# A causal attention kernel's opening, written out slot by slot with fewer weight blocks, and one product for a pair's diagonals

## The chip, the cores and the metric

The kernel runs on one core of a Trainium2 chip. The metric is the device time of one execution in microseconds (us). TensorE is called PE below, VectorE DVE, ScalarE ACT, GpSimd POOL, and SyncE (which issues the DMAs) SP.

## What is computed

Attention with a decaying causal bias on q, k, v of 4 batches, 8 heads, 576 tokens and 64 columns, then two MLPs on the 2304 tokens of 512 columns, with 2048 hidden columns each:

```python
scores = scale * np.matmul(q, k.transpose(0, 1, 3, 2))
cum = np.cumsum(np.log(np.clip(f, 0.0001, 1.0)), axis=-1)
decay = cum[:, :, :, None] - cum[:, :, None, :]
scores = np.where(causal, -1000000000.0, scores + decay)
scores = scores - np.max(scores, axis=-1, keepdims=True)
attn = np.exp(scores)
attn = attn / (np.sum(attn, axis=-1, keepdims=True) + 1e-09)
x = np.matmul(attn, v)                      # then to (tokens, 512)
h = np.maximum(x @ w_in, 0.0)
x = (s * (h * h) + b) @ w_out               # first MLP
h = x @ w_in2
return np.maximum(0.01 * h, h) @ w_out2     # second MLP
```

All inputs are fp32.

## The kernel before

**Units.** The attention is cut into eight units: the first 256 rows of each of the four batches (units 0 to 3), then the other 320 rows of each. A unit has four pairs of heads. For a pair of one of the first units the steps are: S, the scores on PE (q times k, L663 in unit 0 and L300 in units 1 to 3; in unit 0 the decays too, L672; and the mask, L678 or L311); M, the row maxima on DVE (reductions, L684, in unit 0, where the decays are already in the scores; a custom instruction that adds the decays and takes the maximum, L334, in the others); E, the exponentials on ACT with their row sums (L690, L356); D, on DVE, a small addition and a reciprocal (L701 and L702, or L381 and L382) and the diagonal matrices with the reciprocals in them (L715, a product of 128 by 128 for each head and row tile, four for a pair); T, the turn, in which PE multiplies the exponentials by the diagonals and so transposes and scales them at once (L725, twelve products of 128 by 128 for a pair) and ACT copies the result (L710, L387); A, the product with v (L734, eight products); X, the split of the result into a high part (ACT, L748) and a low part (DVE, L749), which is written to `x_all`.

**Weights.** A block of weights (512 KB) is loaded by SP and converted in four instructions or groups: a scaling on ACT (`scale`, L109), a join of three instructions on DVE (`join`, L113, L114, L116), a rounding to the high part on ACT (`high`, L122) and the subtraction of it on DVE (`low`, L126). Each MLP has 32 blocks.

**Stages.** The opening does units 0 and 1, from the start to the first Relu of the first MLP (L952), and converts the first weight blocks on the way. Then come 16 joint steps, which do the first MLP for units 0 and 1 together (L937, L987, 512 columns wide) with unit 2's attention and the rest of the weights' conversion in between. The next units go one by one: in each step one sixteenth of the first MLP of a unit and a piece of a later unit's attention (`attend`, `attend_mid`, `first_mlp`). The second MLP (L1071, L1087) is last.

**What sets the order.** In the opening Tile's scheduler orders each engine by priorities (`ahead`, `run_on`): `first_a`, `first_b`, `first_c` issue S with M and E, D with T, and A with X of unit 0, `first_slots` those of unit 1, so that the two units are interleaved, and `split_to` issues conversions at the lowest priority. From the joint steps on, `in_order` fixes the order on each engine as it is written. There the diagonals of a pair (`diags`, four small instructions and four products) stand at the start of the step after the one that took its exponentials:

```python
        dg.update({k: diags(k) for k in e["turn"]})
```

and the pair's turn stands in that step behind the first product of the MLP (behind the second one in a unit's first step). `W_FIRST` 4, `W_LOAD` 3 and `W_MOST` 18 say how many weight blocks are loaded in the opening; `c_of` says which blocks a joint step converts, from block 8 on, two in a step and one in each third.

Of the kernel before, what the change touches and what calls it, by code (L numbers as in the profile page):

```python
# [8 lines left out]
F32 = mybir.dt.float32  # L9
# [30 lines left out]
def attention_moe_moe_kernel(  # L40
# [51 lines left out]
    class Weights:  # L92
# [35 lines left out]

        def split_to(self, n):
            for k in range(self.done, min(n, len(self.blocks))):  # L130
                self.scale(k)
                self.join(k)
                self.high(k)
                self.low(k)
# [135 lines left out]
    def run_on(first):  # L270
        return nullcontext() if first else tc.high_priority(offset=P_RUN)

    def mm_score(i):

        jb, n, ts, last = tiles[i]
        u, h, j, half = jobs[jb]
        if not half and h % 2:
            return
        b, u0, un, _ = units[u]
        qk = qk_p[j // 2]  # L280
        qn = q_cols(u)
        ps = s_t[i] = ps_a.tile([P, 2, 512], F32, tag="ps_s", name="ps_s", bufs=1)
        if half:
            w = (u0 + un) // 2
            for c in range(2):
                with run_on(c == 0):
                    nc.tensor.matmul(
                        ps[:, c, :w], qk[:, UN:qn], qk[:, qn + c * w : qn + (c + 1) * w], start=True, stop=c == 0
                    )
            with run_on(False):  # L290
                nc.tensor.matmul(ps[:, 1, w - NL : w], ident_h, mask_l, start=False, stop=True)
            return
        s_t[i + 1] = ps
# [26 lines left out]
    def score_max(i):  # L320
# [4 lines left out]
        sm = sm_t[i] = ap.tile([P, 10], F32, tag="sm", name="sm", bufs=4)  # L325
# [39 lines left out]
    def st_split(i):  # L365
        jb, n, ts, last = tiles[i]
        dg = diags(i)
        ps = ps_o.tile([P, 512], F32, tag=f"o{2 + i % 2}", name="ps_t1")
        turn(ps, t_t.pop(i), dg)
        p_t[i] = turned(i, ps)  # L370

# [7 lines left out]
    def diags(i):  # L379
        sm = sm_t.pop(i)  # L380
        nc.vector.tensor_scalar(sm[:, 4:6], sm[:, 2:4], 1.0e-9, None, ALU.add)  # L381
        nc.vector.reciprocal(sm[:, 6:8], sm[:, 4:6])  # L382
        return row_parts(i), diag(i, {t: sm[:, 6 + r : 7 + r] for r, t in enumerate(tiles[i][2])})
# [50 lines left out]
    kept = {}  # L434
# [4 lines left out]

    def st_av(i):  # L440
        jb, n, ts, last = tiles[i]
        u, h, j, half = jobs[jb]
        b, u0, un, _ = units[u]
        if h % 2:
            first_x(u, h // 2, pair_av(u, i))
# [5 lines left out]
    def av_mm(i):  # L451
# [7 lines left out]
        for t in ts:  # L459
# [3 lines left out]
            for e in range(P // m):  # L463
                for k in range(nk):
                    for l in range(2):
                        with run_on(t == ts[0] and e == k == l == 0):
                            nc.tensor.matmul(  # L467
                                av[:, at + e * m : at + (e + 1) * m],
                                v_st[j + e][:, k].rearrange("p l d -> p (l d)"),
                                pt[:, to + l * nk + k, e * m : (e + 1) * m],  # L470
                                start=(k == 0 and l == 0),
                                stop=(k == nk - 1 and l == 1),
                            )
# [25 lines left out]
    def av_end(i):  # L499
# [16 lines left out]
    def split_later():  # L516
        while later and later[0][0] <= read[0] + 2:
            u, pr, raw, inv = later.pop(0)
            with ahead(P_X):
                split_x1(xs[u], pr, raw, inv)  # L520
# [25 lines left out]
    P_ATT, P_AV, P_G, P_W, P_F, P_X = 150, 90, 0, -300, 0, 100  # L546
    P_RUN = 4000

    def ahead(n):
        return tc.high_priority(offset=n)  # L550

    LAG = 2
    NCUM = 3
    U1 = 2
    W_FIRST = 4
    W_LOAD = 3
    W_MOST = 18
    XL = 10

    def slot_c(i):  # L560
        if 0 <= i - 1 < NTL:
            st_split(i - 1)

    def slot_d(i):
        if 0 <= i - LAG < NTL:
            st_av(i - LAG)

    def slot_b(i):
        if i < NTL:
            jb, n, ts, last = tiles[i]  # L570
            st_score(i)
# [9 lines left out]
    qk_0 = []  # L581
    f_sb = ap.tile([P, S], F32, tag="tt", name="f_sb", bufs=4)[:BH]
    cum = ap.tile([P, S], F32, tag="tt", name="cum", bufs=4)[:BH]
    nc.sync.dma_start(out=f_sb, in_=f)
    nc.scalar.preload_act_table_set("natural_log_exp_and_others")
    for r in range(ND // 2):
        qk_0.append(wp.tile([P, 2, 2 * un0], F32, tag="w", name="qk_0"))
        for e in range(2):
            nc.sync.dma_start(out=qk_0[r][:, e], in_=qk0[2 * r + e])
        if r == 0:  # L590
            for _ in range(W_FIRST):
                w1.load(nc.sync)
# [15 lines left out]
    cl = wp.tile([P, 2 * DM], F32R, tag="w", name="cum_hl")  # L608
    for a in range(P // BH):
        nc.gpsimd.tensor_scalar(  # L610
            cl[a * BH : (a + 1) * BH, S : S + H],
            ident[a * BH : (a + 1) * BH, a * BH : a * BH + H],
            -INV,
            0.0,
            ALU.mult,
            ALU.add,
        )
    nc.gpsimd.tensor_copy(ident_h, ident)
    nc.gpsimd.memset(mask_h, 0.0)
    nc.gpsimd.affine_select(  # L620
        out=mask_h,
        in_=mask_h,
        pattern=[[-1, P]],
        compare_op=ALU.is_ge,
        fill=MASK,
        base=0,
        channel_multiplier=1,
    )
    nc.gpsimd.memset(mask_l, 0.0)
    for e in range(2):  # L630
        nc.gpsimd.affine_select(
            out=mask_l[e * D : (e + 1) * D],
            in_=mask_l[e * D : (e + 1) * D],
            pattern=[[-1, NL]],
# [5 lines left out]
    nc.vector.tensor_scalar(f_sb, f_sb, 1.0e-4, 1.0, ALU.max, ALU.min)  # L640
    nc.scalar.activation(f_sb, f_sb, AF.Ln)
    nc.vector.tensor_tensor_scan(cum, f_sb, f_sb, 0.0, ALU.add, ALU.bypass)
    nc.scalar.copy(cl[:BH, :S], cum)
    nc.vector.tensor_tensor(
        out=cl[BH : 2 * BH, :S], in0=cum, in1=cl[:BH, :S].bitcast(F32), op=ALU.subtract
    )
    nc.gpsimd.tensor_scalar(f_sb, cum, -INV, 0.0, ALU.mult, ALU.add)
    nc.sync.dma_start(out=cumd, in_=f_sb)
    nc.gpsimd.tensor_scalar(cl[D:, :un0], cl[:D, :un0].bitcast(F32), 1.0, 0.0, ALU.mult, ALU.add)

    e_0, sm_0, pt_0 = {}, {}, {}
    xs.update({u: x_all[:, u % 2] for u in range(NU)})

    def first_a(p):
        qk = qk_0[p // 2][:, p % 2]
        ps = [ps_o.tile([P, 512], F32, tag=f"o{e}", name="ps_s0") for e in range(2)]
        ex = e_0[p] = wp.tile([P, 2 * DM], F32, tag="w", name="e_0")
        sm = sm_0[p] = ap.tile([P, 5, 2 * NT0], F32, tag="sm_0", name="sm_0", bufs=3)
        parts = [(t, P * t * (t + 1) // 2, (t + 1) * P, e) for t in range(NT0) for e in range(2)]
# [664 lines left out]
```

## Time and profile before

| what | value |
| --- | --- |
| median of 3 runs | 1014.13 us (1011.58 to 1014.45) |
| the profiled execution | 1013.08 us |
| its span in the profile | 1011.2 us |
| PE busy | 982.7 us (97%) |
| DVE busy | 528.4 us (52%) |
| ACT busy | 507.0 us (50%) |
| POOL busy | 27.7 us (3%) |
| PE's mean granted clock | 0.998 of full |

Busy time is the time in which an engine executes an instruction; a share is of the whole span, over stages that differ. Where PE is busy all the time, only its own work counts; in a stage where it isn't, the wait that ends last before each of its instructions does. In a timeline's row the bracket behind an instruction gives the idle time of its engine before it and what ended it. The granted clock is a share of PE's full speed: 1.00 is 2.4 GHz, 0.50 is 1.2 GHz.

### The profile page before, as it was taken

Reading aid. Unit: us, or ns where it says so; the run is one execution under the profiler, and the core shown is the slowest. Engines: PE = TensorE matmul, PEld = TensorE weight load, DVE = VectorE, ACT = ScalarE, POOL = GpSimd, SP = SyncE. Lnnn points to the kernel's source line nnn. Section 1 sums busy time; section 2 is a strip of 40 time slices with the busy share of each in tenths; the row PEclk is TensorE's granted clock in tenths of the full one; section 3 lists DMA queues with packets and bytes.
Section 4 is the critical chain, followed back from the end, with each engine's and each line's share of the span. In section 5 each row is a group of like instructions: output and inputs, shape, how many; then the busy total and the mean of one; then the engine's idle time right before and its main releaser. Section 6 shows DMA issues by size and latency. Waiting matters only on the chain.

```text
span 1011.2 us, 17155 instructions
## 1 busy us (share of the span) xinstructions
PE 982.7 (97%) x6464; PEld 836.5 (83%) x6464; DVE 528.4 (52%) x1383; ACT 507.0 (50%) x1196; POOL 27.7 (3%) x100
## 2 busy tenths in 40 slices
PE   5899999999999999999999999999999999999998
PEld 4667777888888888888999998888888888888887
DVE  6888774367777777777512479785112111211121
ACT  4777665567667677676643556552121222212132
POOL 1000000000000000000000000000000000000000
PEclk9999999999999999999999999999999999999999
DMA  9834022379999899898400695003000100100010
GB/s 298 301 124 174 22 84 84 90 130 199 173 188 201 178 177 202 171 182 186 87 22 1 214 376 202 0 1 123 3 1 1 63 0 1 42 1 1 1 42 21
DMA packets 157075, 110.32 MB, mean 109 GB/s; under 512 B 110593, under 2 KB 135169, under 8 KB 156993
## 3 DMA queue, kind: packets, MB, share of 16 engines
q1 hardware_dynamic: 156992, 109.23, 42.9%
q8 instruction: 51, 0.84, 0.3%
q14 instruction: 32, 0.25, 0.1%
HBM read 74.00 MB, written 10.04 MB: 83 GB/s over the span
## 4 chain that ended last, share of the span: by engine, by line
PE 51%; ACT 0%; DVE 0%; issue 0%
PE ps_o L1087 20%; PE ps_h L1071 20%; PE ps_o L987 6%; PE ps_h L937 6%; PE ps_v L467 0%; DVE o L1099 0%; ACT tt L356 0%; ACT p_hl L410 0%; DVE g L970 0%; ACT g L968 0%; ACT ps_h L967 0%; ACT ps_h L966 0%
## 5 line engine op out<-in xcount | busy, mean ns | idle before, releaser
L937 PE MATMUL ps_h<-x_all,w 128*128 128x256 f32 (+1 forms) x1536 | 231.7, 299 | 2.3 <-ACT r_all L952 0.7
L987 PE MATMUL ps_o<-g,w 128*128 128x256 f32 (+2 forms) x1536 | 231.3, 300 | 0.0
L1087 PE MATMUL ps_o<-w,g 128*128 128x512 f32 x864 | 215.0, 395 | 0.0
L937 PEld LDWEIGHTS ps_h<-x_all,w 128*128 128x128 f32 x1536 | 201.9, 189 | 15.4 <-DVE g L970 3.9
L1071 PE MATMUL ps_h<-x,w 128*128 128x512 f32 (+1 forms) x960 | 213.5, 370 | 0.0
L987 PEld LDWEIGHTS ps_o<-g,w 128*128 128x128 f32 x1536 | 203.1, 189 | 10.7
L1071 PEld LDWEIGHTS ps_h<-x,w 128*128 128x128 f32 x960 | 169.1, 188 | 34.4
L1087 PEld LDWEIGHTS ps_o<-w,g 128*128 128x128 f32 x864 | 161.0, 188 | 37.6
L1079 DVE TENSOR_TENSOR g<-ps_h,g 128x512 fp32r<-128x512 f32 (+1 forms) x80 | 50.9, 637 | 248.9 <-ACT g L1078 248.6
L1077 ACT ACTIVATE ps_h<-ps_h 128x512 f32<-128x512 f32 (+1 forms) x80 | 43.1, 539 | 263.1 <-PE ps_h L1071 263.1
L356 ACT ACTIVATE tt<-tt,sm 128x512 f32<-128x512 f32 (+4 forms) x128 | 76.1, 597 | 77.9 <-DVE sm L334 77.9
L970 DVE TENSOR_TENSOR g<-ps_h,g 128x256 fp32r<-128x256 f32 x112 | 47.1, 420 | 91.4 <-ACT g L968 91.1
L966 ACT ACTIVATE ps_h<-ps_h 128x256 f32<-128x256 f32 x112 | 40.9, 365 | 51.8 <-PE ps_h L937 51.7
L334 DVE CUSTOM_DVE_ANT_0 tt<-ps_s,cumk 128x512 f32<-128x512 f32 (+4 forms) x128 | 59.1, 499 | 4.9 <-DMA cumk<-cumd 2.8
L415 DVE SCALAR_TENSOR_TENSOR p_hl<-tt,sm,p_hl 128x512 f16<-128x512 f32 (+1 forms) x64 | 44.8, 700 | 15.5 <-ACT p_hl L410 15.0
L1078 ACT CAST g<-ps_h 128x512 fp32r<-128x512 f32 (+1 forms) x80 | 43.6, 545 | 6.5 <-PE ps_o L1087 4.1
L300 PE MATMUL ps_s<-qk_p 64*128 64x512 f32 (+3 forms) x224 | 44.5, 493 | 1.7 <-DVE sm L334 0.9
L114 DVE SCALAR_TENSOR_TENSOR wt<-w_raw,wt 128x512 int32<-128x512 int32 x64 | 44.3, 692 | 2.0
L410 ACT ACTIVATE p_hl<-tt,sm 128x512 f16<-128x512 f32 (+1 forms) x64 | 42.6, 665 | 4.2 <-ACT tt L356 3.0
L968 ACT CAST g<-ps_h 128x256 fp32r<-128x256 f32 x112 | 41.8, 373 | 4.4
L109 ACT ACTIVATE wt<-w_raw 128x512 f32<-128x512 f32 x64 | 41.3, 675 | 3.7 <-DMA w_raw<-in_moe_w_in 2.8
L967 ACT ACTIVATE ps_h<-ps_h 128x256 f32<-128x256 f32 x112 | 41.2, 368 | 3.7
(115 smaller groups left out, 783.1 us busy)
## 6 DMA issues: line engine op xcount, KB each, us to landing
w_raw<-in_moe_w_in SPq DMA_DIRECT2D x32, 512.0 KB, 8.3
w_raw<-in_moe_w_out SPq DMA_DIRECT2D x32, 512.0 KB, 9.0
cumk<-cumd SPq DMA_DIRECT2D x32, 256.0 KB, 3.9
qk_p<-in_qk SPq DMA_DIRECT2D x16, 480.0 KB, 4.7
cumk<-cumd SPq DMA_DIRECT2D x32, 144.0 KB, 3.3
v_raw<-in_v SPq DMA_DIRECT2D x16, 288.0 KB, 3.3
out<-o SPq DMA_DIRECT2D x18, 256.0 KB, 2.1
x2r<-x1d SPq DMA_DIRECT2D x4, 1024.0 KB, 5.6
```

Source lines behind the costliest of these rows:

```text
L114: nc.vector.scalar_tensor_tensor(x, top, -0x80000000, x, ALU.bitwise_and, ALU.bitwise_or)
L300: nc.tensor.matmul(ps[:, e, at[r] : at[r + 1]], qk[rows, q0 - u0 : q0 - u0 + m], qk[rows, qn : qn + q0 + m], start=(r == 0), stop=False,)
L334: nc.vector.tensor_tensor_reduce(tt[:, at + k0 : at + k0 + kw], ps[:, c, :kw] if half else ps[:, h % 2, at : at + w], cumk[jb][:, k0 : k0 ...
L356: nc.scalar.activation(e, e, AF.Exp, bias=sm[:, r : r + 1], scale=-1.0, accum_out=sm[:, 2 + r : 3 + r])
L415: nc.vector.scalar_tensor_tensor(v[:, 1, :w], e, inv, v[:, 0, :w], ALU.mult, ALU.subtract)
L937: nc.tensor.matmul(ps, wi[:, a, d * P : (d + 1) * P], x_all[:, :, c, d] if joint[0] else x[:, c, d], start=(d == 0 and n == 0), stop=(d == ...
L970: nc.vector.tensor_tensor(out=g[:, 1, :UN], in0=ps, in1=g[:, 0, :UN].bitcast(F32), op=ALU.subtract)
L987: nc.tensor.matmul(po[d], wo[:, a, d * P : (d + 1) * P], g[:, c], start=(first and n == 0), stop=(last and n == 2),)
L1071: nc.tensor.matmul(ps[:, :n], wi[:, a, d * P : (d + 1) * P], x[:, e, d, :n], start=(d == 0 and k == 0), stop=(d == ND - 1 and k == 2),)
L1078: nc.scalar.copy(g[:, 0, :n], raw)
L1079: nc.vector.tensor_tensor(out=g[:, 1, :n], in0=raw, in1=g[:, 0, :n].bitcast(F32), op=ALU.subtract)
L1087: nc.tensor.matmul(po[m], g[:, a, m * P : (m + 1) * P], wo[:, e, :], start=(i == 0 and k == 0), stop=(i == NF - 1 and k == 2),)
```

## The change

The opening is no longer left to the scheduler. It is written out in ten slots inside `in_order`, so that every engine takes its instructions as written. Slots 0 to 3 hold the four pairs of unit 0, slots 4 to 7 those of unit 1. Slot s issues S, M and E of pair s, then D and T of pair s-1, then the conversions that a table gives for this slot, with A and X of pair s-2 among them. Six blocks are converted by the end (before: eight, and two more were joined), 12 are loaded ahead (before 18). Blocks 0 and 1 are converted in the first slots, 2 and 3 in slots 1 to 6, 4 and 5 in slots 7 to 9; `c_of` starts with block 6. Scores of even slots go to other PSUM banks than those of odd slots. The loads are interleaved otherwise: the first pair's q and k, then two weight blocks, then the rest.

The four diagonals of a pair are made by one product of 512 columns (`pair_diag`), in units 0 to 3. The row sums of a pair's two heads share a tile. For unit 3 the diagonals are made in the step that took the exponentials (`attend_early`, behind the rounding of the MLP's hidden columns), no longer at the start of the next.

```diff
+    def pair_diag(n, sm, ts):
+        nc.vector.tensor_scalar(sm[:, :, 4:6], sm[:, :, 2:4], 1.0e-9, None, ALU.add)
+        nc.vector.reciprocal(sm[:, :, 6:8], sm[:, :, 4:6])
+        t = ap.tile([P, 5 * P], F32, tag=("p_t0", "p_hl_t")[n % 2], name="diag", bufs=1)[:, : 2 * NT0 * P]
+        t = t.rearrange("p (e t c) -> p e t c", e=2, t=NT0)
+        nc.vector.tensor_tensor(
+            out=t,
+            in0=ident_h.unsqueeze(1).unsqueeze(1).to_broadcast([P, 2, NT0, P]),
+            in1=sm[:, :, 6:8].unsqueeze(3).to_broadcast([P, 2, NT0, P]),
+            op=ALU.mult,
+        )
+        return [{k: t[:, e, r] for r, k in enumerate(ts)} for e in range(2)]
...
-    W_MOST = 18
+    W_MOST = 12
...
+    FIRST = [(u, p) for u in range(2) for p in range(H // 2)]
+    SLOTS = len(FIRST)
+    convert = {
+        0: ((), (1,), (0, 1), ()),
+        1: ((0, 1), (), (), (2,)),
+        2: ((), (2,), (2,), ()),
+        3: ((2,), (), (), ()),
+        4: ((), (), (), (3,)),
+        5: ((), (3,), (3,), ()),
+        6: ((3,), (), (), ()),
+        SLOTS - 1: ((), (), (), (4, 5)),
+        SLOTS: ((), (4, 5), (4, 5), ()),
+        SLOTS + 1: ((4, 5), (), (), ()),
+    }
...
+        nc.vector.tensor_tensor_scan(cum, f_sb, f_sb, 0.0, ALU.add, ALU.bypass)
+        w1.scale(0)
+        nc.scalar.copy(cl[:BH, :S], cum)
+        nc.vector.tensor_tensor(
+            out=cl[BH : 2 * BH, :S], in0=cum, in1=cl[:BH, :S].bitcast(F32), op=ALU.subtract
+        )
+        w1.scale(1)
+        nc.gpsimd.tensor_scalar(cl[D:, :un0], cl[:D, :un0].bitcast(F32), 1.0, 0.0, ALU.mult, ALU.add)
...
+    def pair_scores(s):
+        u, p = FIRST[s]
+        if s % 2:
+            ps = [ps_o.tile([P, 512], F32, tag=f"o{e}", name="ps_s0") for e in range(2)]
+        else:
+            both = ps_a.tile([P, 2, 512], F32, tag="ps_s", name="ps_s0", bufs=1)
+            ps = [both[:, e] for e in range(2)]
...
+    with in_order():
+        setup()
+        for s in range(SLOTS + 2):
+            if s < SLOTS:
+                pair_scores(s)
+            if 1 <= s <= SLOTS:
+                pair_turn(s - 1)
+            lows, joins, highs, scales = convert.get(s, ((), (), (), ()))
+            for b in lows:
+                w1.low(b)
+            for b in joins:
+                w1.join(b)
+            if s >= 2:
+                pair_x(s - 2)
+            for b in highs:
+                w1.high(b)
+            for b in scales:
+                w1.scale(b)
...
+            load_more(1 + s % 2)
...
-        dg.update({k: diags(k) for k in e["turn"]})
...
-    def attend_tail(n):
+    def attend_early(n):
+        diags(at_step(n)["diag"])
...
-    c_of = turns(8, [(i, 1 if i % 3 == 2 else 2) for i in range(NF)])
+    c_of = turns(6, [(i, 1 if i in (2, 5, 8) else 2) for i in range(NF)])
...
-        while len(w1.blocks) < min(2 * NF - 2 * (i < 11), W_MOST + 2 * i + 2):
+        while len(w1.blocks) < min(2 * NF - 2 * (i < 12), W_MOST + 2 * i + 2):
```

Three places show the order on an engine, before and now. The names in the rows are the tiles written and read; numbers behind them tell buffers apart. Of PE in the middle of the opening, before: the units alternate, and turns and products with v stand wherever the scheduler put them.

```order
L734 MATMUL av_363<-p_hl,v_106 64x256
L734 MATMUL av_363<-p_hl,v_106 64x128 x2
L734 MATMUL av_454<-p_t,v_116 64x256
L725 MATMUL ps_t_375<-diag,e_288 128x128 x3
L725 MATMUL ps_t_384<-diag,e_288 128x128 x3
L725 MATMUL ps_t_448<-diag,tt 128x128 x3
L734 MATMUL av_487<-p_hl,v_106 64x256 x2
L734 MATMUL av_487<-p_hl,v_106 64x128 x2
L725 MATMUL ps_t_420<-diag,tt 128x128 x3
L725 MATMUL ps_t_499<-diag,e_392 128x128 x3
```

Now (slots 6 and 7; L759 is the turn, L767 the product with v, L680 the scores, L688 the mask):

```order
L759 MATMUL ps_t_490<-diag,e_409 128x128 x3
L759 MATMUL ps_t_496<-diag,e_409 128x128 x3
L767 MATMUL av_503<-p_hl,v_154 64x256 x2
L767 MATMUL av_503<-p_hl,v_154 64x128 x2
L680 MATMUL ps_s_510<-qk_p 128x128
L680 MATMUL ps_s_511<-qk_p 128x128
L680 MATMUL ps_s_510<-qk_p 128x256
L680 MATMUL ps_s_511<-qk_p 128x256
L688 LDWEIGHTS ident_h
L688 MATMUL ps_s_510<-mask_h,ident_h 128x128
```

Each slot now has the same order on PE: the scores of a pair, the turn of the pair before it, the product with v of the pair before that.

Of DVE in the opening, before: the reciprocals and diagonals (L701, L702, L715) of a pair of unit 0, with a conversion and the maxima of a head of unit 1 behind them.

```order
L701 TENSOR_SCALAR sm_393<-sm_393 128x4
L702 RECIPROCAL sm_393<-sm_393 128x4
L715 TENSOR_SCALAR diag<-ident_h,sm_393 128x128 x4
L126 TENSOR_TENSOR w<-w_raw,w 128x512
L334 ISA tt,sm<-ps_s,cumk 128x256
L334 ISA sm 128x1
L334 ISA tt,sm<-ps_s,cumk 128x128
L334 ISA sm 128x1
L381 TENSOR_SCALAR sm<-sm 128x2
```

Now (slot 6; L696 is the custom instruction with its read of the maximum, here the last two of the pair's):

```order
L696 ISA e_470,sm_471<-ps_s_461,cumk 128x128
L696 ISA sm_471 128x1
L696 ISA e_470,sm_471<-ps_s_461,cumk 128x256
L696 ISA sm_471 128x1
L367 TENSOR_SCALAR sm_410<-sm_410 128x2x2
L368 RECIPROCAL sm_410<-sm_410 128x2x2
L371 TENSOR_TENSOR diag<-ident_h,sm_410 128x512
L126 TENSOR_TENSOR w<-w_raw,w 128x512
L782 TENSOR_TENSOR x_all<-av_503,x_all 128x256
```

The maxima of the slot's own pair stand ahead of the diagonals of the pair before it; conversions and the low part of X follow.

Of DVE in the first step of unit 3's attention, before: the diagonals stand behind two scalings of the joint MLP's output (L1017).

```order
L334 ISA tt,sm<-ps_s,cumk 128x128
L334 ISA sm 128x1
L970 TENSOR_TENSOR g<-ps_h,g 128x256
L1017 TENSOR_SCALAR x1o<-ps_o,sb 128x512
L1017 TENSOR_SCALAR p_hl<-ps_o,sb 128x512
L381 TENSOR_SCALAR sm<-sm 128x2
L382 RECIPROCAL sm<-sm 128x2
L715 TENSOR_SCALAR diag<-ident_h,sm 128x128 x2
```

Now (L968 was L970, L1015 was L1017):

```order
L325 ISA tt,sm_1537<-ps_s,cumk 128x128
L325 ISA sm_1537 128x1
L367 TENSOR_SCALAR sm_1537<-sm_1537 128x2x2
L368 RECIPROCAL sm_1537<-sm_1537 128x2x2
L371 TENSOR_TENSOR diag<-ident_h,sm_1537 128x512
L968 TENSOR_TENSOR g<-ps_h,g 128x256
L1015 TENSOR_SCALAR x1o<-ps_o,sb 128x512
L1015 TENSOR_SCALAR p_hl<-ps_o,sb 128x512
```

The diagonals of the pair have moved ahead of the subtraction of the hidden columns and of the two scalings.

## Rows read from the trace of the kernel before

**Rows 1.** Busy time by stretch: stretch, its length, busy us (instructions) of each engine, clock, DMA.

```profile
30.00:40.00 10.00, 6.71 (x56) 5.10 (x55) 7.58 (x38) 7.77 (x29) 0.00 (x0) 1.00 1.04 359
...
61.00:160.00 99.00, 99.00 (x492) 78.12 (x494) 73.88 (x172) 67.90 (x141) 0.00 (x0) 1.00 0.24 80
```

**Rows 2.** Timeline of PE, opening: start, length, line, operation, tiles, count [idle before, releaser].

```profile
9.10 0.79 PE L672 MATMUL ps_s<-cum_hl 64*128 64x128 f32 x3 [1.10 <-POOL cum_hl L649]
...
14.85 1.68 PE L663 MATMUL ps_s<-qk 64*128 64x128 f32 x7 [4.42 <-ACT e L690]
...
17.32 0.61 PE L678 MATMUL ps_s<-mask_h,ident_h 128*128 128x128 bf16 x4
...
19.84 2.88 PE L725 MATMUL ps_t<-diag,e 128*128 128x128 f32 x12
22.65 1.34 PE L663 MATMUL ps_s<-qk 64*128 64x128 f32 x8
...
24.14 0.40 PE L678 MATMUL ps_s<-mask_h,ident_h 128*128 128x128 bf16 x4
```

**Rows 3.** Timeline of all engines, set-up.

```profile
6.03 0.75 DVE L644 TENSOR_TENSOR cum_hl<-cum,cum_hl 32x576 fp32r<-32x576 f32 x1 [0.74 <-ACT cum_hl L643]
...
7.66 0.66 ACT L109 ACTIVATE wt<-w_raw 128x512 f32<-128x512 f32 x1 [1.66 <-DMA w_raw<-in_moe_w_in]
...
8.43 0.61 POOL L649 TENSOR_SCALAR cum_hl<-cum_hl 64x256 fp32r<-64x256 f32 x1
```

**Rows 4.** Timeline of DVE, first unit.

```profile
8.35 0.43 DVE L113 TENSOR_SCALAR wt<-wt 128x512 int32<-128x512 int32 x1 [1.58 <-ACT wt L109]
...
9.62 0.69 DVE L116 SCALAR_TENSOR_TENSOR w_raw<-w_raw,wt 128x512 int32<-128x512 int32 x1
...
15.29 0.17 DVE L701 TENSOR_SCALAR sm<-sm 128x4 f32<-128x4 f32 x1 [0.53 <-ACT e L690]
...
15.78 0.88 DVE L715 TENSOR_SCALAR diag<-ident_h,sm 128x128 f32<-128x128 bf16 x4
16.57 1.29 DVE L126 TENSOR_TENSOR w<-w_raw,w 128x512 fp32r<-128x512 f32 x2
17.86 1.15 DVE L684 TENSOR_REDUCE sm<-ps_s 128x1 f32<-128x128 f32 x4
```

**Rows 5.** Timeline of PE, opening, at the full clock.

```profile
33.22 0.92 PE L300 MATMUL ps_s<-qk_p 64*128 64x256 f32 x8 [0.76 <-PE ps_s L678]
34.08 0.40 PE L311 MATMUL ps_s<-mask_h,ident_h 128*128 128x128 bf16 x4
...
35.20 1.60 PE L725 MATMUL ps_t<-diag,e 128*128 128x128 f32 x12
...
47.59 0.89 PE L734 MATMUL av<-p_hl,v 128*64 128x256 f32 x8
```

**Rows 6.** Timeline of DVE, maxima of a pair of unit 3.

```profile
160.94 0.42 DVE L334 CUSTOM_DVE_ANT_0 tt<-ps_s,cumk 128x256 f32<-128x256 f32 x1
...
162.06 0.08 DVE L334 DVE_READ_ACCUMULATOR2_ANT sm<- 128x1 f32 x1
```

**Rows 7.** Timeline of PE, a wait and what followed.

```profile
39.28 0.94 PE L725 MATMUL ps_t<-diag,tt 128*128 128x128 f32 x6 [2.47 <-ACT p_hl L710]
...
41.22 1.65 PE L725 MATMUL ps_t<-diag,tt 128*128 128x128 f32 x6
```

**Rows 8.** Busy time and granted clock in stretches of 1 us.

```profile
41.00:42.00 1.00, 1.00 (x7) 0.78 (x4) 0.88 (x6) 0.70 (x3) 0.00 (x0) 0.50 1.03 371
```

**Rows 9.** Timeline of all engines, end of the opening.

```profile
59.00 0.41 DVE L749 TENSOR_TENSOR x_all<-av,x_all 128x256 fp32r<-128x256 f32 x1
...
60.25 0.60 ACT L952 ACTIVATE r_all<-ps_h 128x512 f32<-128x512 f32 x1 [1.35 <-PE ps_h L937]
```

**Rows 10.** Waits of PE from 160 to 200: for what, total, times, longest.

```profile
PE ps_t L725 <- DVE diag L715: 2.7, 4, 1.7
```

**Rows 11.** Timeline of ACT, end of a pair's exponentials in unit 3.

```profile
163.09 0.19 ACT L356 ACTIVATION_READ_ACCUMULATOR tt<-tt,sm 128x1 f32 x1
```

More of the change, by code (lines that the diff above doesn't have):

```diff
@@ L127, in low @@
             self.done = n + 1
[L129 to L134, printed above, removed]
         def get(self, i):
@@ L432, in tail_hl, with in_order @@
         return kept["tail"]
-    kept = {}
+    kept, dg, sm_0 = {}, {}, {}
+    engines = {e.engine for e in (nc.tensor, nc.vector, nc.scalar, nc.gpsimd, nc.sync)}
+    before, carry, ended = {}, [], []
+    @contextmanager
+    def in_order():
+        cur = nc.cur_bb.bb.instructions
+        n = len(cur)
+        yield
+        info = mybir.DependencyInfo(mybir.DependencyClass.NoSync, mybir.DependencyReason.DATA)
+        for i in cur[n:]:
+            if i.engine in engines:
+                if i.engine in before:
+                    tc.add_manual_dep(i, before[i.engine], info, reason="in order")
+                before[i.engine] = i.name
     def pt_tile(n, dt, w):
@@ L620, in attention_moe_moe_kernel, with wide, load_first @@
[L620 to L630, printed above, removed]
+    def wide(name, dt=F32):
+        return wp.tile([P, 2 * DM], dt, tag="w", name=name)
+    def load_first(r, e):
+        if e == 0:
+            qk_0.append(wide("qk_0").rearrange("p (e c) -> p e c", e=2))
+        nc.sync.dma_start(out=qk_0[r][:, e], in_=qk0[2 * r + e])
@@ L651, in attention_moe_moe_kernel @@
[L651 to L659, printed above, removed]
+        nc.vector.tensor_scalar(f_sb, f_sb, 1.0e-4, 1.0, ALU.max, ALU.min)
@@ new lines, in setup @@
+        nc.sync.dma_start(out=cumd, in_=f_sb)
+        nc.gpsimd.memset(mask_l, 0.0)
+        for e in range(2):
+            nc.gpsimd.affine_select(
+                out=mask_l[e * D : (e + 1) * D],
+                in_=mask_l[e * D : (e + 1) * D],
+                pattern=[[-1, NL]],
+                compare_op=ALU.is_ge,
+                fill=MASK,
+                base=0,
+                channel_multiplier=1,
+            )
+        for p in range(2):
+            load_pair(p)
+        for k in range(NCUM):
+            load_cumk(k)
@@ new lines, in setup @@
+        first_v(1)
+        w1.join(0)
+    parts = [(t, P * t * (t + 1) // 2, (t + 1) * P, e) for t in range(NT0) for e in range(2)]
+    PC = P * NT0 * (NT0 + 1) // 2
+    qk_0, v_in, pair = [], {}, {}
+    cl = wide("cum_hl", F32R)
+    def pair_scores(s):
[5 more added lines that the diff above has]
+            ps = [both[:, e] for e in range(2)]
+        qk, kc = (qk_p[p], UN) if u else (qk_0[p // 2][:, p % 2], un0)
@@ L703, in first_b, with pair_turn @@
+    def pair_turn(s):
+        ex, sm = pair.pop(s)
+        two = pair_diag(s, sm, range(NT0))
+        at = {t: a for t, a, *_ in parts}
+        pair[s] = []
         for e in range(2):
-            n = 2 * p + e
-            at = {t: P * t * (t + 1) // 2 for t in range(NT0)}
-            dg = diag(e, {t: sm[:, 4, e * NT0 + t : e * NT0 + t + 1] for t in range(NT0)})
             ps = ps_o.tile([P, 512], F32, tag=f"o{2 + e}", name="ps_t0")
-            turn(ps, ex[:, e * PC : (e + 1) * PC], (at, dg))
@@ L720, in turn, with pair_x @@
+    def pair_x(s):
+        u, p = FIRST[s]
+        if s == SLOTS - 1:
+            av = ps_o.tile([P, 512], F32, tag="o0", name="av_0")
+        elif s % 2 and s < SLOTS - 2:
+            av = ps_h.tile([P, 512], F32, tag="h", name="av_0")
+        else:
+            av = ps_a.tile([P, 512], F32, tag="ps_v", name="av_0", bufs=1)
+        first_x(u, p, first_av(u, p, pair.pop(s), av))
+    def turn(ps, e, at, dg):
         to = 0
@@ L796, in attention_moe_moe_kernel @@
     plan = {}
     def at_step(n):
-        return plan.setdefault(n, {k: [] for k in ("v", "early", "s", "av", "x", "turn", "first", "load")})
+        return plan.setdefault(n, {k: [] for k in ("v", "early", "s", "av", "x", "turn", "diag", "first", "load")})
     t_of = {}
```

374 lines of the change are left out of this document (146 added, 228 removed).

## The prediction

> **What bounds the kernel now.** I read the busy times by stretch first. In the joint steps TensorE (PE) is busy 99.00 of 99 us, VectorE (DVE) 73.88 and ScalarE (ACT) 67.90; in the opening PE is busy only 6.71 us of the ten from 30 to 40 [rows 1]. So a microsecond saved or lost in the opening moves everything behind it, and in the joint steps only PE's own work counts. Next I read PE's timeline and, for what each step costs, DVE's [rows 2 to 6]; then what the clock did after a long wait [rows 7, 8]; then the opening's end, which I put at the first Relu of the joint steps, 60.25 [rows 9]; last, PE's waits behind the opening, of which the change touches four, 2.7 us together, all for a diagonal [rows 10]. The reader is to see a PE-bound kernel with one weakly filled stage of 60 us in front.
>
> Letters for a slot's work on one pair of heads: S scores, M row maxima, E exponentials, D diagonals, T the turn (its product with the diagonals), A the product with v, X the split into high and low parts.
>
> **The sum, step by step.** It is made against the profiled execution, 1013.08 us, which lies 1.05 below the median of the three runs.
>
> *Set-up, +0.5.* S(0) hangs on ACT's copy of the decays, then a subtraction of 0.75 on DVE and a copy of 0.61 on POOL; its decay products started at 9.10, and the POOL copy 8.43 + 0.61 released them [rows 2, 3]. Now the scaling of weight block 0 stands on ACT ahead of that copy, and it waits for its load, which had landed at 7.66 [rows 3]. One 256 KB load fewer is queued ahead of it, so I estimate 6.8 (bounds: 6.0, where the copy stood before, which gives no loss, and 7.66, which gives +1.4). From 6.8: scaling 0.66, copy some 0.67 (its own length, 0.75 on DVE, is near), 0.75, 0.61, so 9.5; then 0.79 of decay products and 0.61 of masks [rows 2]: S(0) ends at 10.9, before at 10.4.
>
> *First two slots, T(0) 3.3 earlier (the 0.5 included).* Before, S(1) waited for the exponentials until 14.85 and lasted to 17.93; T(0) came at 19.84 and took 2.88 [rows 2]. Now S(1) has banks of its own and follows at once: 10.9 + 3.1 = 14.0. On DVE stand M(0), 1.15 + 0.17 = 1.32; a join, 8.35 to 10.31 or some 1.9; M(1); then D(0): 15.29 to 15.78 for the small ones and one product of 512 columns. No such product is in the trace; the nearest is the subtraction of 512, 1.29 for two [rows 4]. Bounds: that 0.65, and the four products it replaces, 0.88; I take 0.65, as the width is the same, so D is 1.14. M(0) ends 12.2, the join 14.1, M(1) 15.4, D(0) 16.55, T(0) at 2.88 ends 19.4, where it ended at 22.7.
>
> *Six full slots, 38.1 long.* PE's queue is now S(s), T(s-1), A(s-2), DVE's is M(s), D(s-1). T(s-1) waits for D(s-1), D(s-1) stands behind M(s), M(s) needs S(s), and S(s+1) stands behind A(s-2). Nothing overlaps: a slot lasts S + M + D + T + A, of which PE stands M + D, some 2.4 us, in one piece. First unit at the full clock: S 22.65 to 24.54, so 1.89; T 1.60; A 0.89 [rows 2, 5]; with 1.32 and 1.14 that is 6.85. Second unit: S 0.92 + 0.34 (33.22 to 34.48) = 1.26 [rows 5], M 160.94 to 162.14 = 1.20 [rows 6], so 1.26 + 1.20 + 1.14 + 1.60 + 0.89 = 6.1. Slots 2 and 3 end at 33.1, slots 4 to 7 at 57.5. Conversions, joins, E and the copies of T lie beside it: they fit in the 3.7 us in which DVE waits for T, A and S. If they did not, a slot would last the rest of a join longer; a join of 1.9 and an X of 0.41 leave 1.4.
>
> *Tail, 8.3.* X(5) (0.41 on DVE and as much on ACT) and D(7) end at 59.5. Behind D(7), two joins (3.8), the rounding of block 5 on ACT (0.66, as its scaling), one subtraction (0.65) and X(7) (0.41) stand in that order; the turn, its copies, A and X need less. X(7) ends at 65.0. Before, the last X began at 59.00 and the Relu followed its end by 0.84 [rows 9]; so now Relu at 65.8. Against 60.25: **+5.5** with PE at its full clock from slot 2 on.
>
> *Clock, +5.* Before, a wait of 2.47 us ended at 39.28; from 41 to 42 the granted clock was 0.50 (1.2 GHz), and a turn of six took 1.65 where one of twelve had taken 1.60 [rows 5, 7, 8]. That dip cost some 0.85 on that turn and, as I estimate, as much on its neighbours, 1.7 in all. After the change seven slots have a wait of about that length (2.4). No dip: 0. A dip behind each: 7 x 1.7 = 12. One row can't say which; a wait a little shorter than the one that brought a dip, with 3.7 us of work between, I put near the middle, three dips, so **+5**. The Trainium skill (TensorE: Matmul & The Clock Gate, section "HAM oscillation — how this bites in real kernels") tells of a kernel whose bursts between long waits each start at half clock; by that rule the term would be the 12. The trace bears it out once [rows 7, 8].
>
> *Diagonals of unit 3, -2.7.* The four waits [rows 10] end. In the first step the exponentials are out at 163.28 [rows 11] and D needs 1.14, so it is done at 164.4; what held it, a subtraction of the hidden columns and in that first step two scalings, now stands behind it. That step alone has 1.7 of the 2.7; the other three have 0.3 each, less than the D that leaves their front. Bounds: 0, if the earlier D delays a subtraction that PE then waits for; 2.7.
>
> *The rest, 0.* Four blocks fewer are converted in the opening: some 2.5 us each of DVE and 1.3 of ACT go to the joint steps, which makes 84 and 73 of 99 [rows 1], still under PE. Cover gone (a step with two blocks and a pair of unit 2): under 1 us. Loads of the last two blocks start one step later; a step lasts 99/16 = 6.2 us and three lie between.
>
> Sum: 1013.1 + 5.5 + 5 - 2.7 = **1021**, 0.7% over the median.
>
> **Rivals.**
> - *Full clock throughout.* The waits stay just too short to bring the clock down, as they are a little shorter than 2.47. For it: the stretch 30 to 40 ran at full clock with PE at two thirds [rows 1]. 1013.1 + 5.5 - 2.7 = 1016.
> - *Half clock in nearly each slot,* as the dip of rows 8. 1013.1 + 5.5 + 12 - 2.7 = 1028. For it: one row out of one.
> - *Faster.* The opening runs at the pace of its busiest engine and not of the chain: DVE has per slot 1.2 + 1.14 + 0.41 and three quarters of a block of 2.5, 4.6 us, if M(s) begins inside S(s) and T and A run under the next M. Six slots of 4.6 for 6.35 save 10.5: first Relu at 55.3, time 1013.1 - 5 - 2.7 = 1005. It decides from a slot of some 5.5 us downwards. Against it: both queues are in program order, and A(s-2) stands behind T(s-1), so PE has nothing to do under D.
> - *The diagonals' gain fails,* as bounded above: 1024.
>
> **How the numbers follow.** About 0.3% (3 us) can be told from no change: 1011.1 to 1017.2. Chances: forecast with two to five dips 0.50, full clock 0.20, half clock nearly throughout 0.17, faster 0.07, diagonals' gain lost 0.06. Full clock lies inside 0.3% for the most part, some of it with a set-up or tail a little longer lies over; so same 0.2, faster 0.07, slower 0.73. The range goes from the full clock with 1.5 off for steps that overlap a little, 1014.5, to half clock in nearly each slot, 1028; outside are the faster rival and what lies beyond 1028.
>
> **What would show it.** First Relu of the joint steps near 71 (66 at full clock, under 61 if I am wrong about the chain); in each slot one PE wait of 2.2 to 2.6 us put down to a diagonal, and T, A, S without a gap; 2.88 for turns of twelve in some slots and 1.60 in others; in the tail the last X behind two joins; no wait for a diagonal at the start of unit 3's steps; from the first Relu to the end 950.2, which is 952.8 (1013.08 - 60.25) less 2.7. If the slot period is below 5.5, or PE's turns don't wait for D, the sum is wrong at its root.

## The result, and the profile after

The changed kernel took 1021.41 us (median of 10 runs, 1015.4 to 1024.25), the kernel before 1012.12 in the runs beside it (10 runs, 1009.97 to 1014.45). The ratio is 1.0087, 95% interval 1.0065 to 1.0109: slower by 0.9%. The profiled execution of the changed kernel is one of its quicker ones, 1018.26 us; that of before was 1013.08.

| profiled execution, us | before | after | difference |
| --- | --- | --- | --- |
| first Relu of the joint steps | 60.25 | 69.83 | +9.58 |
| from there to the end | 952.83 | 948.43 | -4.40 |
| sum | 1013.08 | 1018.26 | +5.18 |

```profile
69.83 0.60 ACT L950 ACTIVATE r_all<-ps_h 128x512 f32<-128x512 f32 x1 [0.57 <-PE ps_h L935]
```

So two effects of opposite sign lie behind the 5.2 of these executions: the opening is 9.6 longer, and what follows is 4.4 shorter.

The opening on PE, from the timeline of the changed kernel (L759 is the turn, L767 the product with v, L680 the scores; columns as in [rows 2]):

```profile
15.37 2.90 PE L759 MATMUL ps_t<-diag,e 128*128 128x128 f32 x12 [3.08 <-DVE diag L371]
...
23.24 1.83 PE L759 MATMUL ps_t<-diag,e 128*128 128x128 f32 x12 [2.42 <-DVE diag L371]
...
31.10 2.77 PE L759 MATMUL ps_t<-diag,e 128*128 128x128 f32 x12 [2.50 <-DVE diag L371]
...
38.67 2.90 PE L759 MATMUL ps_t<-diag,e 128*128 128x128 f32 x12 [2.41 <-DVE diag L371]
...
42.30 0.93 PE L680 MATMUL ps_s<-qk_p 64*128 64x128 f32 x8
...
45.91 1.58 PE L759 MATMUL ps_t<-diag,e 128*128 128x128 f32 x12 [2.35 <-ACT e L723]
...
48.21 0.93 PE L680 MATMUL ps_s<-qk_p 64*128 64x128 f32 x8
...
51.87 2.90 PE L759 MATMUL ps_t<-diag,e 128*128 128x128 f32 x12 [2.40 <-DVE diag L371]
...
59.30 1.58 PE L759 MATMUL ps_t<-diag,e 128*128 128x128 f32 x12 [2.35 <-ACT e L723]
...
63.72 1.57 PE L759 MATMUL ps_t<-diag,e 128*128 128x128 f32 x12 [2.04 <-DVE diag L371]
```

Each turn has a wait in front of it, 2.0 to 2.5 us from the second on, put down to the diagonals or, twice, to ACT's exponentials; there too the turn starts 0.15 us behind the end of the diagonals (45.91, behind 45.07 + 0.69), as it does at 38.67. At the full clock twelve products take 1.58, as in [rows 5]; at 15.37, 31.10, 38.67 and 51.87 they take 2.77 to 2.90. Where the clock stays up, a slot lasts 48.21 - 42.30 = 5.9 us.

DVE in one slot, from its timeline (the first and the last maximum, the small addition of the diagonals, their product of 512 columns):

```profile
42.82 0.42 DVE L782 TENSOR_TENSOR x_all<-av,x_all 128x256 fp32r<-128x256 f32 x1 [4.30 <-ACT x_all L781]
43.54 0.29 DVE L696 CUSTOM_DVE_ANT_0 e<-ps_s,cumk 128x128 f32<-128x128 f32 x1 [0.29 <-PE ps_s L688]
...
44.31 0.42 DVE L696 CUSTOM_DVE_ANT_0 e<-ps_s,cumk 128x256 f32<-128x256 f32 x1
...
44.65 0.17 DVE L367 TENSOR_SCALAR sm<-sm 128x4 f32<-128x4 f32 x1
...
45.07 0.69 DVE L371 TENSOR_TENSOR diag<-ident_h,sm 128x512 f32<-128x512 bf16 x1
```

The maxima come first, 43.54 to 44.65, then the diagonals, 44.65 to 45.76; PE's turn starts at 45.91. DVE had been idle 4.3 us ahead of the X that comes first.

The clock by stretches of 10 us (columns as in [rows 1], PEclk third from the right):

```profile
20.00:30.00 10.00, 6.18 (x42) 4.37 (x40) 5.66 (x16) 3.60 (x12) 0.00 (x0) 0.83 0.73 257
30.00:40.00 10.00, 6.49 (x38) 5.30 (x39) 4.07 (x16) 4.91 (x19) 0.00 (x0) 0.73 0.11 28
40.00:50.00 10.00, 7.12 (x60) 5.16 (x58) 5.22 (x19) 5.83 (x17) 0.00 (x0) 0.93 0.56 181
50.00:60.00 10.00, 5.78 (x38) 4.69 (x39) 4.83 (x22) 4.89 (x19) 0.00 (x0) 0.83 0.56 177
```

Before, the only stretch under 1.00 in the opening was 40 to 50, with 0.83. From 10 to 20 the granted clock reads 1.00 in both kernels, although the first turn runs at half speed there (2.90 now, 2.88 before); that shows only in the lengths of the rows. Behind the opening, PE's turns in unit 3 no longer wait, and their rows are shorter:

```profile
174.58 1.50 PE L759 MATMUL ps_t<-diag,tt 128*128 128x128 f32 x12
...
182.24 1.59 PE L935 MATMUL ps_h<-x_all,w 128*128 128x256 f32 x12
183.66 1.50 PE L759 MATMUL ps_t<-diag,tt 128*128 128x128 f32 x12
...
192.74 1.50 PE L759 MATMUL ps_t<-diag,tt 128*128 128x128 f32 x12
```

In [rows 10] they waited 2.7 us together. The same places before:

```profile
184.46 1.59 PE L937 MATMUL ps_h<-x_all,w 128*128 128x256 f32 x12
186.37 1.70 PE L725 MATMUL ps_t<-diag,tt 128*128 128x128 f32 x12 [0.32 <-DVE diag L715]
...
196.12 1.70 PE L725 MATMUL ps_t<-diag,tt 128*128 128x128 f32 x12 [0.32 <-DVE diag L715]
```

A step of unit 3 is now 192.74 - 183.66 = 9.08 us; before it was 9.75 (196.12 - 186.37).

### The profile page after: what moved, and what is told of

Read it like the earlier page. It is cut to its first block, busy times and chain, and to the rows that moved or that the text cites. A ratio compares the mean times of both kernels' runs of the same rounds, so it can differ in the third digit from the quotient of the medians.

```text
span 1016.4 us, 17056 instructions
## 1 busy us (share of the span) xinstructions
PE 981.4 (97%) x6464; PEld 837.2 (82%) x6464; DVE 524.8 (52%) x1307; ACT 508.3 (50%) x1196; POOL 28.0 (3%) x100
## 4 chain that ended last, share of the span: by engine, by line
PE 51%; ACT 0%; DVE 0%; issue 0%
PE ps_o L1085 20%; PE ps_h L1069 20%; PE ps_o L985 6%; PE ps_h L935 6%; PE ps_v L474 0%; DVE o L1097 0%; ACT tt L347 0%; ACT p_hl L411 0%; DVE g L968 0%; ACT g L966 0%; ACT ps_h L965 0%; ACT ps_h L964 0%
## 5 line engine op out<-in xcount | busy, mean ns | idle before, releaser
L347 ACT ACTIVATE tt<-tt,sm 128x256 f32<-128x256 f32 (+3 forms) x112 | 68.9, 616 | 76.2 <-DVE sm L325 76.2
L968 DVE TENSOR_TENSOR g<-ps_h,g 128x256 fp32r<-128x256 f32 x112 | 47.1, 421 | 86.6 <-ACT g L966 86.6
L325 DVE CUSTOM_DVE_ANT_0 tt<-ps_s,cumk 128x256 f32<-128x256 f32 (+3 forms) x112 | 54.1, 520 | 2.1 <-PE ps_s L297 0.7
L474 PE MATMUL ps_v<-p_t,v_st 128*128 128x128 f16 (+1 forms) x768 | 42.7, 209 | 0.4 <-DMA p_t<-p_hl_t 0.4
```

What stands on the lines that cost most here:

```text
L325: nc.vector.tensor_tensor_reduce(tt[:, at + k0 : at + k0 + kw], ps[:, c, :kw] if half else ps[:, h % 2, at : at + w], cumk[jb][:, k0 : k0 ...
L347: nc.scalar.activation(e, e, AF.Exp, bias=sm[:, r : r + 1], scale=-1.0, accum_out=sm[:, 2 + r : 3 + r])
L968: nc.vector.tensor_tensor(out=g[:, 1, :UN], in0=ps, in1=g[:, 0, :UN].bitcast(F32), op=ALU.subtract)
```

## Experiments

**The theory** is the prediction's: a slot lasts S + M + D + T + A since each queue is in program order and D stands behind M; the waits this makes on PE bring the clock down; unit 3's diagonals give a part back. **The rivals:** the slots are held by conversions, copies or loads; the low clock has nothing to do with the waits; the gain behind the opening comes from the one product and not from the move. First four runs on one chip (kernel before beside them 1011.9, 28 runs), then three more on another (before 1012.93, 7 runs). The changed kernel was not measured again beside them, so differences from its 1021.41 are good to about 1 us, by which the kernel before differs (1011.9 to 1012.93).

### PE's waits filled with idle work

```diff
+        if s:
+            fill = ps_h.tile([P, 512], F32, tag="h", name="fill")
+            for _ in range(20):
+                nc.tensor.matmul(fill[:, :P], ident_h, mask_h, start=True, stop=True)
         ex, sm = wide("e_0"), pair_sm()
```

> The changed kernel with 20 products of the mask by the identity (128 columns, about 0.1 us each at the full clock) behind each pair's scores but the first, into a bank that nobody reads: extra work of PE that fills most of its wait for D. Theory that the waits bring the clock down: granted clock 1.00 from about 20 us on, every turn of twelve at 1.6, first Relu about 5 us earlier (64 to 66), time about 1016. Rival (the dips come from elsewhere): turns at 2.8 stay, and the time is as before or up to 8 us longer for the extra products.

Measured: 1011.37 us (10 runs, 1009.73 to 1014.54), against before 0.9991 (0.9979 to 1.0003). With 140 products more to do the kernel is 10 us shorter than the changed one, where about 5 were expected, and level with before. Its timeline on PE:

```profile
15.34 1.57 PE L763 MATMUL ps_t<-diag,e 128*128 128x128 f32 x12 [0.96 <-DVE diag L371]
...
18.16 1.28 PE L694 MATMUL fill<-mask_h,ident_h 128*128 128x128 bf16 x20
...
38.90 1.58 PE L763 MATMUL ps_t<-diag,e 128*128 128x128 f32 x12 [1.23 <-ACT e L727]
...
41.21 0.93 PE L680 MATMUL ps_s<-qk_p 64*128 64x128 f32 x8
...
47.17 0.93 PE L680 MATMUL ps_s<-qk_p 64*128 64x128 f32 x8
...
55.20 2.32 PE L763 MATMUL ps_t<-diag,e 128*128 128x128 f32 x12 [2.04 <-DVE diag L371]
```

The filler takes 1.28 us (2.34 the first time), waits of 1.2 to 1.4 remain behind it (0.96 the first time), and each turn takes 1.6 but the last one, at 55.20, which has no filler in front of it and takes 2.32. A slot is 47.17 - 41.21 = 5.96, as it was where the clock had stayed up. The first turn starts at the same time in both (15.34, 15.37), and the first Relu comes at 62.87 instead of 69.83. As the slots' other work is the same, these 7 us are, in these two executions, the speed of PE: 1.33 lie in the first turn (1.57 for 2.90), 1.1 in the scores behind it (1.49 for 2.62), and the rest in the turns that the low clock slowed in the changed kernel. This run has a dip of its own behind the last turn, with a granted clock of 0.50 from 56 to 59; the Relu follows the last diagonals by 7.8 there (62.87 behind 54.36 + 0.69), by 6.3 in the changed kernel. Without it the gain of these two executions would be some 8.5.

### Diagonals ahead of the maxima

```diff
         for s in range(SLOTS + 2):
+            if 1 <= s <= SLOTS:
+                pair_dg(s - 1)
             if s < SLOTS:
                 pair_scores(s)
```

(`pair_dg` is the call of `pair_diag`, taken out of `pair_turn`.)

> In each slot the diagonals of pair s-1 are issued on DVE ahead of the maxima of pair s; nothing else is changed. Chain theory (a slot lasts S + M + D + T + A because D stands behind M): PE's waits for a diagonal, 2.4 us in each of eight slots, go almost whole, since D then runs under S; the slot falls from 6.0 to about 4.3, the dips of the clock go with the waits, the first Relu of the joint steps comes at 52 to 57 instead of 69.8, and the time is 1003 to 1008. Rival (conversions, copies or loads hold the slots, and the place of D does not matter): waits stay over 1.5 us, first Relu after 66, time over 1015.

Measured: 1007.39 us (5 runs), against before 0.9966 (0.9953 to 0.9979); first Relu 58.61. The order of two groups of instructions on DVE is worth 14 us against the changed kernel, the dips of the clock that go with the waits included. PE's timeline:

```profile
25.44 1.63 PE L762 MATMUL ps_t<-diag,e 128*128 128x128 f32 x12 [1.92 <-DVE diag L371]
...
35.62 1.58 PE L762 MATMUL ps_t<-diag,e 128*128 128x128 f32 x12 [1.02 <-DVE diag L371]
...
37.93 0.93 PE L680 MATMUL ps_s<-qk_p 64*128 64x128 f32 x8
...
42.57 0.93 PE L680 MATMUL ps_s<-qk_p 64*128 64x128 f32 x8
...
51.17 2.90 PE L762 MATMUL ps_t<-diag,e 128*128 128x128 f32 x12 [3.95 <-DVE diag L371]
```

In unit 1 slots are 42.57 - 37.93 = 4.64 us; four turns in the middle wait 0.5 to 1.1 where the theory had expected almost none, the one at 25.44 waits 1.92 and the last 3.95, so first Relu is 1.6 later than the bound given. Two things hold it: D now stands behind the X of the slot before, which waits for ACT; and the decay rows of the last pair come late:

```profile
43.26 0.42 DVE L785 TENSOR_TENSOR x_all<-av,x_all 128x256 fp32r<-128x256 f32 x1 [1.43 <-ACT x_all L784]
43.60 0.16 DVE L367 TENSOR_SCALAR sm<-sm 128x4 f32<-128x4 f32 x1
...
47.22 0.29 DVE L696 CUSTOM_DVE_ANT_0 e<-ps_s,cumk 128x128 f32<-128x128 f32 x1 [1.96 <-DMA cumk<-cumd]
...
50.33 0.69 DVE L371 TENSOR_TENSOR diag<-ident_h,sm 128x512 f32<-128x512 bf16 x1
```

### The product with v ahead of the turn

```diff
             if s < SLOTS:
                 pair_scores(s)
+            if s >= 2:
+                early_av(s - 2)
             if 1 <= s <= SLOTS:
                 pair_turn(s - 1)
```

(`early_av` is the product with v, taken out of `pair_x`.)

> The changed kernel with the product with v of pair s-2 ahead of the turn of pair s-1 on PE, so that it runs while DVE makes M and D. Chain theory: the wait for a diagonal falls from 2.4 to 1.5 in six slots and the slot by 0.87, so 5 to 6 us; with shorter waits fewer dips of the clock, up to 5 more; first Relu at 59 to 65, time 1008 to 1014. Rival (the slot is held elsewhere): first Relu within 2 us of 69.8.

Measured: 1008.92 us (10 runs), against before 0.9971 (0.9959 to 0.9983); first Relu 60.20. The waits that PE's timeline shows:

```profile
23.67 1.57 PE L763 MATMUL ps_t<-diag,e 128*128 128x128 f32 x12 [1.48 <-DVE diag L371]
...
34.32 1.58 PE L763 MATMUL ps_t<-diag,e 128*128 128x128 f32 x12 [1.60 <-DVE diag L371]
...
39.43 1.58 PE L763 MATMUL ps_t<-diag,e 128*128 128x128 f32 x12 [1.55 <-DVE diag L371]
...
50.03 1.58 PE L763 MATMUL ps_t<-diag,e 128*128 128x128 f32 x12 [1.87 <-DVE diag L371]
```

They fall to 1.5 to 1.9, the slot to 39.43 - 34.32 = 5.1, 0.85 less, and no turn behind the first one runs at half clock. Time and first Relu lie where the theory put them. Here DVE's order is that of the change: the slot is a chain across both queues, and either can open it.

### Unit 3's diagonals, moved alone in the kernel before

```diff
-        dg.update({k: diags(k) for k in e["turn"]})
...
     def attend_tail(n):
+        dg.update({k: diags(k) for k in at_step(n)["diag"]})
```

> The kernel before with one part of the change: unit 3's diagonals (still four products) made in the step that took the exponentials. If the 4.4 us that the changed kernel is shorter behind the first Relu come from this move, this kernel is 4 us faster than before (1008), with no wait of PE for a diagonal from 160 to 200. If the idle time alone counts, 2.7 us (1009.5). Rival (the single product, or the other weight table, brings them): no gain, 1012, as the four small products reach PE just as late.

Measured: 1008.33 us (11 runs) beside 1011.9, ratio 0.9973 (0.9964 to 0.9982), so 1.8 to 3.6 us less. PE has no wait from 160 to 200, with four small products as before; its turns, 9.08 us apart, take 1.50 as after the change:

```profile
174.85 1.50 PE L725 MATMUL ps_t<-diag,tt 128*128 128x128 f32 x12
...
183.93 1.50 PE L725 MATMUL ps_t<-diag,tt 128*128 128x128 f32 x12
```

From the first scores of unit 3 to the end the profiled execution takes 849.3 us (1009.75 - 160.41), before 853.4 (1013.08 - 159.65): 4.1 less. What comes ahead of those scores took 0.8 longer in this execution. The move gives the gain, not the single product.

### Unit 3's diagonals back in the changed kernel

```diff
+        diags(e["turn"])
         if e["first"]:
...
     def attend_early(n):
-        diags(at_step(n)["diag"])
```

> The changed kernel with unit 3's diagonals, still one product, back at the start of the next step. If the move alone brings the 4.4 us behind the first Relu: four waits of PE for a diagonal from 168 to 210, the stretch from the first Relu to the end 952 instead of 948.4, time 1025. If the one product brings them: no such waits, 948.4, and 1021.

Measured: 1026.96 us (4 runs), against before 1.0146 (1.0117 to 1.0174). Four waits are back:

```profile
182.87 1.58 PE L759 MATMUL ps_t<-diag,tt 128*128 128x128 f32 x12 [2.12 <-DVE diag L371]
...
192.91 1.58 PE L759 MATMUL ps_t<-diag,tt 128*128 128x128 f32 x12 [0.74 <-DVE diag L371]
...
202.94 1.58 PE L759 MATMUL ps_t<-diag,tt 128*128 128x128 f32 x12 [0.74 <-DVE diag L371]
```

Three of them are 0.74, where the three short ones of before were 0.32. One product delivers both heads' diagonals at its end, 192.07 + 0.69, and the turn starts at 192.91, 1.25 behind the small addition at 191.66. Of the four small ones the first head's two came first (176.18 to 176.57), and the turn at 176.61 didn't wait for the second head's, which were made from 176.97 on: 0.83 behind the addition at 175.78. The single product is thus worse for PE where somebody waits, and a step is 10.03 us (202.94 - 192.91) against 9.75. From the first Relu, 75.84, to the end this execution took 954.1, more than before and 2 more than expected. Its opening is instruction for instruction that of the changed kernel, and it is 6.0 us longer than in the changed kernel's profile (69.83): from 20 us on, five turns took 2.77 or more and one 2.16, where there it was three and one of 1.83, and the granted clock from 20 us to the first Relu was 0.79, there 0.86. So the same opening costs several us more or less by how often the clock falls. The spread of the changed kernel's ten runs goes with it: the mean granted clock of the whole execution was 0.994 in the shortest (1015.4) and 0.986 in the four longest (1023.13 to 1024.25).

### Loads of the last blocks behind the decay rows

```diff
-            load_more(1 + s % 2)
+            if s < 4 or s == SLOTS:
+                load_more(1 + s % 2 if s < 4 else 3)
```

(on top of the diagonals ahead of the maxima)

> The run with the diagonals ahead of the maxima, and its last three weight loads of the opening issued after slot 7 and not in slots 4 to 6, so that the decay rows of the last pair are not queued behind them. In that run DVE waited 1.96 us for the last pair's rows, PE 3.95 for its diagonal, and the turn behind fell to half clock (2.90 for 1.57). If the queue of loads is the cause: that wait falls to about 1, the turn takes 1.6, first Relu 58.6 less 4 = 54.6, time 1003 to 1004. If not (the rows are late for another reason): as that run, 1007.

Measured: 1005.58 us (4 runs), against before 0.993 (0.9913 to 0.9947); first Relu 57.68. DVE's wait for the rows is gone, so the queue of loads was its cause. The first Relu comes only 0.9 sooner than in the run with the diagonals ahead, where 4 were expected, and the time is above the 1003 to 1004: PE's last turn still waits 2.27, as no scores stand in front of it, and still falls to 2.90; and an earlier turn of this execution does too.

```profile
25.64 2.54 PE L762 MATMUL ps_t<-diag,e 128*128 128x128 f32 x12 [2.11 <-DVE diag L371]
...
50.11 2.90 PE L762 MATMUL ps_t<-diag,e 128*128 128x128 f32 x12 [2.27 <-DVE diag L371]
```

### Diagonals in the pair's own slot

```diff
+            if s < SLOTS:
+                pair_dg(s)
             if s >= 2:
                 pair_x(s - 2)
+            if s > SLOTS:
+                for b in lows:
+                    w1.low(b)
```

(on top of the run before; `pair_dg(s - 1)` at the slot's start is gone, and blocks 4 and 5 are scaled in slot 6, joined in 7 and 8)

> As the run before it in this call, but a pair's diagonals are made in its own slot, behind its maxima and ahead of the low part of X, and the conversion of blocks 4 and 5 starts a slot earlier with its last subtractions behind the last X. Chain theory: the turn of pair s finds its diagonals when its place comes, slots fall to PE's own S + T + A or the DVE's work, 3.8 to 4.6 us, the clock stays up, first Relu at 50 to 53, time 999 to 1002. If ACT's exponentials and copies hold the slots in its place, slots stay at 4.6 and the time at 1003.

Measured: 1000.7 us (4 runs, 999.22 to 1001.29), against before 0.9887 (0.9869 to 0.9904): 1.1% faster than before, 2% than the change as it was, with all its parts together. First Relu at 50.02. PE's timeline:

```profile
30.38 0.93 PE L680 MATMUL ps_s<-qk_p 64*128 64x128 f32 x8
...
31.66 1.58 PE L762 MATMUL ps_t<-diag,e 128*128 128x128 f32 x12
...
33.96 0.93 PE L680 MATMUL ps_s<-qk_p 64*128 64x128 f32 x8
...
38.36 0.93 PE L680 MATMUL ps_s<-qk_p 64*128 64x128 f32 x8
...
39.64 1.58 PE L762 MATMUL ps_t<-diag,e 128*128 128x128 f32 x12
...
43.95 1.58 PE L762 MATMUL ps_t<-diag,e 128*128 128x128 f32 x12 [1.93 <-DVE diag L371]
```

Where the diagonals stand behind no join, a turn can follow the scores at once, and a slot is 33.96 - 30.38 = 3.6 us, PE's own work (the turn at 31.66). Behind a join PE waits 0.8 (1.9 at 43.95, where no scores stand in front), and one turn waits 1.0 because the exponentials of its pair come late; such slots are 4.4 to 4.6. All waits in front of turns together are 6.3 us, against 19.5 in the changed kernel, and the granted clock is 1.00 in each ten us from 20 on.

## Why the prediction came out as it did

The direction was right, and so was the mechanism: the chain across the two queues, the waits, and the clock behind some of them. That the time, 1021.41 against 1021 forecast, came out to 0.4 us is luck: three terms of the sum were mis-sized, and the errors cancel. Against the profiles:

| term of the sum | forecast | measured |
| --- | --- | --- |
| first Relu, clock up but for the first turn | 65.8, +5.5 | some 62.6, +2.4 |
| clock | +5 | +7.2 in the profile, some +10 by the medians |
| behind the first Relu | -2.7 | -4.4 |
| time | 1021 | 1018.26 profiled, 1021.41 median |

The 62.6 comes from the run with the waits filled: 62.87, plus 1.33 for its faster first turn, less 1.56 for the dip behind its last turn. The clock is what is left, 69.83 - 62.6. The median lies 3.15 above the profiled execution, and as the runs' length goes with their granted clock, I put that to the clock too; 1021.41 - 1011.37 = 10.0 against the filled run says much the same. So the first and the third term came out 4.9 lower together, and the clock took some 5 more than forecast.

*Set-up, too long by 1.1.* I put the landing of the first weight block at 6.8, bounds 6.0 to 7.66, S(0)'s end at 10.9 and the turn's end at 19.4. ACT's scaling started at 5.63, S(0) ended at 9.74, and T(0) ran from 15.37 to 18.27. The lower bound was wrong: I took one load less in the queue as worth 0.8 us, and the block came 2.0 sooner. The scaling did push ACT's copy back, from 5.32 to 6.19, yet the decay products came sooner than before (8.41 for 9.10): before, POOL was busy with other work until 8.35 and only then made its copy, so S(0) did not hang on ACT's copy there, as the step has it.

*Slots, right as a chain, 1.8 too long in all.* 6.1 were forecast for the second unit at the full clock, 5.9 to 6.0 measured; 6.85 for the first, 6.2 to 6.3 with the waits filled (23.05 - 16.84). The first unit's S was read from a row that began at half speed: 1.89, where S(2) of the filled run takes 1.49. PE stands 2.35 to 2.5 in one piece in each, forecast 2.4. The two runs that opened the chain, on DVE or on PE, show that it is one: slots of 4.6 and 5.1, and 14 and 12.5 us less in time, with no instruction taken away. The "faster" rival of the prediction, that DVE's and PE's work overlap, wasn't in the change and is what the last version does: its slots are 3.6 to 4.6, below the 5.5 from which that rival was to decide.

*Tail, right.* D(7) ended at 63.5 and the Relu followed 6.3 later, as forecast (59.5 and 65.8), with the last X behind two joins and two subtractions (one was counted, but the joins took less than the 3.8).

*Clock, too small.* The step said that three of seven waits bring a dip of 1.7 each, and that S(2) runs at the full clock. S(2) did not (1.1 of the 7.2). In the profile three of the seven turns from 23.24 on run at half clock and one in part, some 1.5 each with what follows them; in the other profile of the same opening five and one. So of 14 waits of 2.0 to 2.5 us, 8 had a slow turn behind them, and two a partly slow one. With the waits at 1.2 to 1.4 (filled) or 1.5 to 1.9 (product with v ahead), no turn that had such a wait was slow. In the other runs a wait of 1.93 had no slow turn behind it, one of 1.92 a product with v of 1.55 for 0.87, one of 2.04 a turn of 2.32, and those of 2.11, 2.27 and 3.95 turns of 2.54 to 2.90. The row of before, one wait and one dip, was thus better evidence than the middle that I took. The Trainium skill (TensorE: Matmul & The Clock Gate, section "HAM oscillation — how this bites in real kernels") tells of bursts that each start slow after a long wait; here somewhat more than half of them did, and the 12 that I worked out for that rule is nearer to the 10 of the medians than my 5 is.

*Unit 3's diagonals, mis-sized.* I counted the idle time in the waits, 2.7. But a step fell by 9.75 - 9.08 = 0.67 where its idle time had been 0.32: behind a wait the turn no longer overlaps with the product ahead of it (1.91 from the product at 184.46 to the turn at 186.37, now 1.42 from 182.24 to 183.66), and the turn's own row is 1.70 instead of 1.50. Three steps at 0.67 and the first at 2.06 (the 4.67 from 162.20 to 166.87 are 2.81, and the turn 0.20 less) make 4.1 of the 4.4; the other 0.3 are as much as one wait for a maximum less, later.

*The rest at nothing, right.* From the first Relu to the last of the joint steps it is 96.7 us before (60.25 to 156.94) and 96.7 after (69.83 to 166.51). The step counted four blocks more to convert in them; there are two, 26 roundings and subtractions instead of 24. In 99 us from just behind the first Relu DVE is busy 78.7 us, forecast 84, and ACT 70.2, forecast 73.

## What to carry to other kernels

Where an order is written by hand, every engine's queue is a promise about the others: with the scores of pair s and the turn of pair s-1 on PE, the diagonals of s-1 must not stand behind the maxima of s on DVE. Draw the chain across the queues before counting busy time; here two groups swapped were worth 14 us, and each diagonal in its own slot, with loads and conversions moved too, 20. A wait of PE cost more than its idle time here: the overlap with the product ahead (0.35 on 0.32 of idle), and in some cases the clock behind it; where the wait can't go, a little idle work in it may pay.

## What the runs showed that I had not expected

- Work that nobody reads made the changed kernel 10 us faster: with 20 products of 128 columns in seven slots, 1.28 us each time, the granted clock was 1.00 (2.4 GHz) from 10 to 50 us.
- The same opening, instruction for instruction, ended at 69.83 in one profile and at 75.84 in another. The ten runs of this kernel spread from 1015.4 to 1024.25.
- One product of 512 columns, 0.69 us on DVE, replaced four of together 0.88, and still made PE wait longer (0.74 for 0.32) where the turn waits for it, because the first head's diagonals came with the second's.
